# Skip factors of a state-space block: four columns become four rows before they go to DRAM, and the loads of them move

## The chip, the cores and the metric

The kernel runs on one core of a Trainium2 chip. The metric is the device time of one execution in microseconds, smaller is better. Three runs of the kernel before gave 994.62, 995.08 and 999.35 us; the median is 995.08.

## The reference

A block of two parts on 2048 tokens of width 640, with a modulation computed from a conditioning vector `c`:

```
mod = (silu(c) @ w_mod)                       # sa, ca, ga, sb, cb, gb, each 640 long
h = layernorm(x) * (1 + ca) + sa
x = x + ga * A(h)                             # A: long convolution by FFT, plus h * Dskip
h = layernorm(x) * (1 + cb) + sb
x = x + gb * B(h)                             # B: (h Wg * h Wu) Wd

K[d, l] = Re sum_n C[d,n] * exp(dt[d]*(A_re + i A_im)[d,n] * l) * dt[d]*B[d,n]
A(h) = causal convolution of h with K, plus h * Dskip
```

`Dskip` is added to tap 0 of the convolution kernel, scaled as the kernel itself is (by `ga` and `1 + ca`). These scaled values are the skip factors.

## The kernel before

The work has two big stages. Up to about 480 us the kernel generates the convolution kernels K and runs the FFT convolution of part A; behind that, the matmuls of part B. The channels go in five blocks of 128, NB = 5. K is generated in 40 steps n of 16 channels each: GpSimd builds phase and magnitude tables (Ph, EQ, EP: L710), ScalarE takes absolute values and sines of them (ab, tra, trb: all ScalarE work stands at L230, in a helper), VectorE multiplies (QtA, PtA, QtB, PtB: L765 to L792), TensorE multiplies the halves (kg: L807 and L822) and adds the skip factors of every second step by one matmul of `dskt` with the identity (L811).

Each step has three groups, and between the groups stand slots for side jobs. A job has due times in the table SCHED; a slot runs the jobs that are due in order of their numbers. So the order of instructions on each engine is written at build time, and each engine works through its list in order. An instruction that waits holds everything behind it on its engine. SP issues nearly all transfers in this way, in one list.

Side jobs that matter here:

- `mod_l` and `u_modr`/`u_modc`: load a 1600 KB piece of `w_mod` into t_tw or t_ti (L353) and multiply it with silu(c) (L360).
- `u_stats`: load rows of A_u into buffers gha, ghb, ghc and others (L465), take their statistics on VectorE (L473). `row_stats` makes reciprocal standard deviations of them (L276 to L283).
- `u_hm`: normalise those rows on ScalarE and store them in DRAM as `hm` (L485); rows whose buffer had to be given away are loaded again first (L465 too). A buffer can be loaded again only when its store has landed.
- `u_pre`: load `hm` back, transposed by the access pattern (L856), and start the FFT.
- `u_fold`, due at 157, 189, 197 and 222: TensorE turns modulation rows into columns (L379), VectorE combines them (L384 to L396), among them the skip factors `dcol[:, 1:]`, 128 channels by 4 blocks. SP stores these in DRAM, `dgd` (L397). TensorE then spreads the columns sh and gg over all rows by products with the identity (L403, L404), and ScalarE copies the results from PSUM into shr and f16a.
- `dskip(j)`, four jobs: load `dgd` into partition 32 j of `dskt`, 32 runs of 4 values each (L413). Channel block 0 (n below 8) uses values loaded at the start; the blocks behind it need these loads from n = 9 on.
- `u_k`: the first FFT step of a finished K (L844), copied to f16b by ScalarE.

A transfer of a column layout such as `dgd[P:].rearrange("(b p) -> p b")` moves single values of 4 bytes.

Of the kernel before, what the change touches and what calls it, by code (L numbers as in the profile page):

```python
# [18 lines left out]
P = 128  # L19
D = 640  # L20
# [3 lines left out]
NB = D // P  # L24
# [46 lines left out]
    tab=(487, 829),  # L71
    fo=(157, 189, 197, 222),
    e0=(138,),
    ds=(205, 222, 503, 397),
    mc=((-872, 289, 307, 356, 356), (217, 378, 439, 446, 461), (309, 570, 620)),
    q=(
# [148 lines left out]
def tile_kernel(ctx: ExitStack, tc: tile.TileContext, I, out):  # L225
    nc = tc.nc
    V, S, G, PE, SY = nc.vector, nc.scalar, nc.gpsimd, nc.tensor, nc.sync

    def act(o, i, f=AF.Copy, **kw):
        return S.activation(o, i, f, **kw)  # L230
# [12 lines left out]
    ident = const.tile([P, P], F32, name="ident")  # L243
# [17 lines left out]
    def ring(pool, shape, name, dtype=F32):  # L261

        return pool.tile(shape, dtype, name=name + next(slot[name]), bufs=1)
# [3 lines left out]
    def mark(*k):  # L267
        done[k] = done.get(k, 0) + 1

    def need(n, *k):  # L270

        assert done.get(k, 0) >= n, k
# [63 lines left out]
    tv0, tv1 = (ring(fp, [P, 1024], "TV") for _ in range(2))  # L336
    CH = (slice(0, 384), slice(384, D))
    row = [[tv0[0:1, 0:384], tv0[0:1, 384:D]], [tv1[0:1, 0:384], tv1[0:1, 384:D]], [tv0[0:1, D:], tv1[0:1, D : D + 256]]]
    mcol = kconst.tile([P, 5, NB], F32, name="mcol")
    dcol = kconst.tile([P, NB], F32, name="dcol")  # L340
    dgd = dram1.tile([D], F32, name="dgd")
# [31 lines left out]
    def u_fold():  # L373

        need(6, "row")
        pc = ring(ps_f, [P, 512], "psf")
        for m in range(3):
            for b in range(NB):
                PE.matmul(pc[:, m * NB + b : m * NB + b + 1], row[m][b // 3][:, b % 3 * P : b % 3 * P + P], ident[0:1, 0:1], start=True, stop=True)  # L379
        yield  # L380
        p3 = pc[:, : 3 * NB].rearrange("p (m b) -> p m b", m=3)
        sg, rg, g1, sh, gg = (mcol[:, i, :] for i in range(5))
        gp_, gq = pc[:, 16 : 16 + NB], pc[:, 24 : 24 + NB]
        V.tensor_scalar(gp_, p3[:, 1], 1.0, 2.0, op0=OP.add, op1=OP.mult)  # L384
        V.tensor_scalar(sg, gp_, 0.0, 0.5, op0=OP.is_ge, op1=OP.subtract)
        V.tensor_tensor(gp_, gp_, sg, op=OP.mult)
        V.tensor_scalar(gp_, gp_, 1e-20, 2.0, op0=OP.max, op1=OP.mult)
        V.tensor_tensor(g1, gp_, sg, op=OP.mult)
        V.tensor_tensor(gp_, gp_, sg, op=OP.mult)
        V.reciprocal(rg, gp_)  # L390
        V.tensor_tensor(gq, p3[:, 2], g1, op=OP.mult)
        V.tensor_tensor(gg[:, 0:1], p3[:, 2, 0:1], g1[:, 0:1], op=OP.mult)
        V.tensor_tensor(sh[:, 1:], p3[:, 0, 1:], rg[:, 1:], op=OP.mult)
        V.scalar_tensor_tensor(sh[:, 0:1], p3[:, 0, 0:1], rg[:, 0:1], gg[:, 0:1], op0=OP.mult, op1=OP.mult)
        V.tensor_tensor(dt2[:, 1:], gq[:, 1:], dt2[:, 1:], op=OP.mult)
        V.tensor_tensor(dcol[:, 1:], gq[:, 1:], dcol[:, 1:], op=OP.mult)  # L396
        SY.dma_start(dgd[P:].rearrange("(b p) -> p b", p=P), dcol[:, 1:])  # L397
        mark("gg")
        yield
        pt, ps = (ring(ps_f, [P, 512], "psf") for _ in range(2))  # L400
        for b in range(NB):
            o = pt[:, 0:P] if b == 0 else ps[:, (b - 1) * P : b * P]
            PE.matmul(o, sh[:, b : b + 1].to_broadcast([P, P]), ident, start=True, stop=True)  # L403
        PE.matmul(pt[:, P : 2 * P], gg[:, 0:1].to_broadcast([P, P]), ident, start=True, stop=True)  # L404
        yield
        act(shr[:, 0:P], pt[:, 0:P])
        act(xa[:, 4, 0:P], pt[:, P : 2 * P])
        act(shr[:, P:], ps)
        mark("sh")

    def dskip(j):
        need(1, "gg")
        SY.dma_start(dskt[32 * j : 32 * j + 1, 8:], dgd[P:].rearrange("(o t j l) -> o j t l", o=1, j=4, l=4)[:, j])  # L413
        mark("dsk")

# [855 lines left out]
    at(T0["tab"][:1], once(tables))  # L1271
    at(T0["tab"][1:], once(tables_b))
    at(T0["fo"], u_fold)
    at(T0["e0"], once(lambda: LATE.pop()()))
    for j in range(4):
        at(T0["ds"][j : j + 1], once(dskip), j)
# [375 lines left out]
    for r in range(3):  # L1652
        b = (1, 13, 25)[r]
# [192 lines left out]
```

## Time and profile before

| | before |
|---|---|
| runs | 994.62, 995.08, 999.35 us |
| median | 995.08 us |
| profiled execution, its time | 996.15 us |
| profiled execution, its span | 994.4 us |
| granted TensorE clock, mean | 0.95 |
| busy PE, DVE, ACT, POOL | 90%, 73%, 58%, 51% |
| shares of the chain that ended last | PE 55%, DVE 14%, ACT 12%, issue 10%, DMA 6%, POOL 2% |
| moved | 188.54 MB in 159337 packets, 10352 of them under 512 B |

The span is counted from the first to the last instruction; the time has some 1.75 us more around it. Rows of a timeline give start, duration, engine, line, operation, output and inputs, and in square brackets how long the engine was idle before and what ended that. SPq is SP's list of transfers: its durations are those of issuing, and "DMA" in a chain is the time from the issue to the landing. PE, DVE, ACT and POOL are TensorE, VectorE, ScalarE and GpSimd; PEld is TensorE's weight load. Line numbers in the text are those of the kernel before.

### The profile page before, as it was taken

To read this page: it belongs to the slowest core of one execution; us is meant where nothing else is said; L and a number is where in the kernel's file an instruction comes from. 1 tells how busy PE (TensorE), PEld (TensorE's weight loads), DVE (VectorE), ACT (ScalarE), POOL (GpSimd) and SP (SyncE) were. 2 spreads that over 40 slices of the span, in tenths; PEclk is the share of its full clock that TensorE was granted. 3 is DMA by queue.
4 is the path that set the end of the run, shared out by engine and by line. 5 is a ranking of instruction groups with operands and counts; after the bars stand their busy time and mean duration, and the time that the engine had idled before them with its cause. 6 is when DMAs were issued, how large, how long until landed. Compare 5 with 4: busy or idle time off the path is not lost.

```text
span 994.4 us, 26747 instructions
## 1 busy us (share of the span) xinstructions
PE 893.7 (90%) x11120; PEld 725.3 (73%) x11120; DVE 729.1 (73%) x1408; ACT 577.0 (58%) x1071; POOL 510.8 (51%) x400
## 2 busy tenths in 40 slices
PE   4867898899889689998877999999999999999998
PEld 3565656676576567777635888889999788888998
DVE  8798569889989887894758655566677656568952
ACT  4869989886978878772345333334455443435430
POOL 5978899799779989950030254440113122222110
PEclk9877889899889889999999899999999999999999
DMA  8728654555246443667685565724564577658875
GB/s 262 257 54 303 219 186 136 177 167 173 77 153 194 138 123 121 188 214 236 208 230 202 172 214 187 238 92 147 155 241 114 193 228 236 217 181 290 238 239 186
DMA packets 159337, 188.54 MB, mean 190 GB/s; under 512 B 10352, under 2 KB 128880, under 8 KB 158064
## 3 DMA queue, kind: packets, MB, share of 16 engines
q1 hardware_dynamic: 150000, 155.51, 48.8%
q0 software_dynamic: 4752, 21.63, 7.5%
q10 hardware_dynamic: 4464, 9.70, 2.6%
q8 instruction: 87, 1.43, 0.6%
q14 instruction: 34, 0.28, 0.1%
HBM read 124.22 MB, written 62.59 MB: 188 GB/s over the span
## 4 chain that ended last, share of the span: by engine, by line
PE 55%; DVE 14%; ACT 12%; issue 10%; DMA 6%; POOL 2%; SPq 1%; DVEq 0%; POOLq 0%; ACTq 0%
PE pa L1074 17%; PE pa L1508 9%; PE psg L1074 8%; PE psfc L889 2%; PE kg L822 2%; PE kg L807 2%; PE psfa L889 2%; ACT L230 1%; PE psfb L889 1%; ACT trb L230 1%; DMA TVa<-WD 1%; PE psfb L946 1%; PE pa L1560 1%; ACT tra L230 1%; PE psfc L946 1%
## 5 line engine op out<-in xcount | busy, mean ns | idle before, releaser
L1051 POOL TENSOR_TENSOR tf<-wur,wgb 128x256 f32<-128x256 f32 x23 | 18.2, 792 | 251.7 <-DVE wtl L1022 204.5
L710 POOL TENSOR_TENSOR EQ<-LQ,RH 128x1536 f32<-128x1536 f32 x40 | 124.2, 3105 | 9.8 <-DVE QtB L767 9.6
L1022 DVE TENSOR_TENSOR wtl<-tf,wth 128x256 fp32r<-128x256 f32 (+1 forms) x72 | 36.6, 509 | 58.9 <-ACT wth L230 58.9
L710 POOL TENSOR_TENSOR Phb<-LH,DH 128x1536 int32<-128x1536 int32 x20 | 62.3, 3114 | 13.5 <-ACT tra L230 13.5
L710 POOL TENSOR_TENSOR EP<-LP,RH 128x768 f32<-128x768 f32 x40 | 66.0, 1651 | 0.0
L710 POOL TENSOR_TENSOR Pha<-LH,DH 128x1536 int32<-128x1536 int32 (+1 forms) x21 | 62.4, 2971 | 2.9 <-ACT trb L230 2.6
L1508 PE MATMUL pa<-wsg,sh 128*128 128x384 f32 (+1 forms) x304 | 58.6, 311 | 0.0
L822 PE MATMUL kg<-QtB,PtB 64*32 64x64 f32 x2560 | 48.5, 229 | 5.9 <-DVE QtB L766 5.3
L822 PEld LDWEIGHTS kg<-QtB,PtB 64*32 64x32 f32 x2560 | 41.5, 114 | 16.0 <-issue 7.1
L1508 PEld LDWEIGHTS pa<-wsg,sh 128*128 128x128 f32 x304 | 45.8, 189 | 0.0
L1547 POOL DMA_DIRECT2D wsg<-wdc x21 | 11.2, 532 | 66.5 <-PE pa L1560 35.5
L1022 DVE TENSOR_TENSOR wsg<-wga,wsg 128x640 fp32r<-128x640 f32 x36 | 32.9, 920 | 11.9 <-ACT wsg L230 11.9
L1074 PE MATMUL pa<-sh,wth 128*128 128x512 f32 x112 | 35.3, 397 | 6.5 <-DVE a L1423 6.1
L1022 DVE TENSOR_TENSOR sl<-a,sh 128x512 fp32r<-128x512 f32 x53 | 36.7, 712 | 5.8 <-ACT sh L230 5.8
L230 ACT ACTIVATE sh<-a 128x512 fp32r<-128x512 f32 x53 | 32.0, 622 | 14.9 <-PE psg L1560 6.2
L230 ACT ACTIVATE a<-pa 128x512 f32<-128x512 f32 x12 | 7.2, 597 | 54.7 <-PE pa L1074 54.7
L230 ACT ACTIVATE wsg<-wga 128x640 fp32r<-128x640 f32 x36 | 26.1, 729 | 21.7 <-PE pa L1508 11.0
L230 ACT ACTIVATE wth<-tf 128x256 fp32r<-128x256 f32 (+1 forms) x72 | 32.2, 479 | 9.8 <-PE pa L1074 5.3
L1074 PE MATMUL pa<-hh,wsg 128*128 128x512 f32 x136 | 36.7, 395 | 0.5 <-DVE wsg L1022 0.5
L1139 POOL TENSOR_SCALAR hfa<-xb,hr,hr 128x128 f32<-128x128 f32 x4 | 2.3, 572 | 67.6 <-DVE hr L283 67.6
L230 ACT ACTIVATE s<-pa 128x512 f32<-128x512 f32 x11 | 6.6, 598 | 49.4 <-PE pa L1074 49.4
L765 DVE TENSOR_TENSOR QtA<-tra,EQ 128x1024 f32<-128x1024 f32 x20 | 24.4, 1221 | 14.8 <-PE kg L807 9.2
(665 smaller groups left out, 3143.8 us busy)
## 6 DMA issues: line engine op xcount, KB each, us to landing
wsg<-wdc POOLq DMA_DIRECT2D x21, 640.0 KB, 5.1
wgb<-B_w_gate SPq DMA_DIRECT2D x24, 320.0 KB, 4.7
wur<-B_w_up SPq DMA_DIRECT2D x24, 320.0 KB, 6.0
wsd<-wsg SPq DMA_DIRECT2D x12, 640.0 KB, 3.9
wga<-wdg SPq DMA_DIRECT2D x12, 640.0 KB, 4.6
wsg<-wsd POOLq DMA_DIRECT2D x12, 640.0 KB, 4.7
wdc<-xb SPq DMA_DIRECT2D x21, 320.0 KB, 4.2
TVb<-WD SPq DMA_DIRECT2D x22, 256.0 KB, 3.5
```

What stands on the lines that cost most here:

```text
L230: return S.activation(o, i, f, **kw)
L710: G.tensor_tensor(o.rearrange("p x (h l) -> p x h l", l=8), lo.unsqueeze(2).to_broadcast([P, rows, nh, 8]), hi.rearrange("p h x -> p x h") ...
L765: return [lambda: V.tensor_tensor(Qt[:, :, :, 0:32], tr[:, :, :, ::-1], e[:, :, 0:32].unsqueeze(1).to_broadcast([P, 2, R, 32]), op=OP.mult ...
L807: PE.matmul(kg[j * 32 : j * 32 + 32, dd, :], PtA[:, c, dl * 4 + j, :], QtA[:, c, dl * 4 + j, :], start=dd == 0 and c == 0, stop=False, til ...
L822: PE.matmul(kg[j * 32 : j * 32 + 32, dd, :], PtB[lo : lo + 64, c, r, :], QtB[lo : lo + 64, c, r, :], start=False, stop=dd == 7 and c == 1, ...
L889: PE.matmul(r[c][par * 64 : par * 64 + 64, i, :], t_tw[:, k0 + k, c, :], src[:, k, :], start=True, stop=True, tile_position=(0, par * 64))
L946: PE.matmul(r[par][:, i], t_ti[lo : lo + 64, qd * 4 + i, c, :], x[lo : lo + 64, c, i, :], start=c == 0, stop=c == 1, tile_position=(lo, 0))
L1022: V.tensor_tensor(lo, v, hi, op=OP.subtract)
L1051: E.tensor_tensor(t[:, 0:2], u[:, 0:2], g[:, 0:2], op=OP.subtract)
L1074: PE.matmul(ps, w[a][:, k], x[b][:, l], start=first and n == 0 and m == 0, stop=n == 2 and m == len(ks) - 1, skip_group_check=True)
L1508: PE.matmul(AC[tb][t][c], x[:, ts], w[:, cs], start=st, stop=f == NF - 1 and n == 2 and (c == 0 or t % 2 == 1))
L1547: G.dma_start(WD[q], wdc[:, q // 3, q % 3])
```

## The change

The store of the skip factors moves from the second piece of `u_fold` to its last one. Before it TensorE multiplies `dcol[:, 1:]` with the identity into four rows of 128 values, next to the products of L403 and L404, and ScalarE copies these rows from PSUM into a free part of buffer TVb. The store then has four pieces of 512 bytes. The due times of the four loads change from 205, 222, 503, 397 to 250, 255, 397, 411.

```diff
-    ds=(205, 222, 503, 397),
+    ds=(250, 255, 397, 411),
...
+    drow = tv1[0 : NB - 1, D + 256 : D + 256 + P]
...
         V.tensor_tensor(dcol[:, 1:], gq[:, 1:], dcol[:, 1:], op=OP.mult)
-        SY.dma_start(dgd[P:].rearrange("(b p) -> p b", p=P), dcol[:, 1:])
         mark("gg")
         yield
...
         PE.matmul(pt[:, P : 2 * P], gg[:, 0:1].to_broadcast([P, P]), ident, start=True, stop=True)
-        yield
+        PE.matmul(pt[0 : NB - 1, 2 * P : 3 * P], dcol[:, 1:], ident, start=True, stop=True)
+        yield
+        act(drow, pt[0 : NB - 1, 2 * P : 3 * P])
+        SY.dma_start(dgd[P:].rearrange("(b p) -> b p", p=P), drow)
+        mark("dg")
         act(shr[:, 0:P], pt[:, 0:P])
...
     def dskip(j):
-        need(1, "gg")
+        need(1, "dg")
```

On SP, at the place where `u_fold` ends, this stood in a row before (the last row is the load that waits for the store of ghc):

```order
L397 DMA dgd<-dcol 128x4x1
L413 DMA dskt<-dgd 1x32x4
L353 DMA t_tw<-w_mod 128x5x640
L413 DMA dskt<-dgd 1x32x4
L465 DMA ghb<-A_u 128x640
L485 DMA hm<-f16a 128x640
L485 DMA hm<-Wb 128x640
L485 DMA hm<-Wa 128x640
L485 DMA hm<-ghc 128x640
L465 DMA ghc<-A_u 128x640
```

And this stands there now (the lines of the changed file are four further down, `TVb` is the buffer with the four rows):

```order
L354 DMA t_tw<-w_mod 128x5x640
L408 DMA dgd<-TVb 4x128
L469 DMA ghb<-A_u 128x640
L489 DMA hm<-f16a 128x640
L489 DMA hm<-Wb 128x640
L417 DMA dskt<-dgd 1x32x4
L489 DMA hm<-Wa 128x640
L417 DMA dskt<-dgd 1x32x4
L489 DMA hm<-ghc 128x640
L469 DMA ghc<-A_u 128x640
```

The load of t_tw is now ahead of the store, three transfers stand between the store and the first load of it where none stood, and the first two loads stand among the stores of `hm`. The other two loads, which stood nine transfers apart, now stand together at the place of the first.

On TensorE, the rows of `u_fold` before, with the products of a finished step around them:

```order
L403 MATMUL psfb<-ident,mcol 128x128
L403 MATMUL psfc<-ident,mcol 128x128 x4
L404 MATMUL psfb<-ident,mcol 128x128
L822 MATMUL kg<-QtB,PtB 32x64 x32
L844 MATMUL psfb<-ct,Kta 64x128 x8
```

And now:

```order
L403 MATMUL psfb<-ident,mcol 128x128
L403 MATMUL psfc<-ident,mcol 128x128 x4
L404 MATMUL psfb<-ident,mcol 128x128
L405 MATMUL psfb<-ident,dcol 4x128
L826 MATMUL kg<-QtB,PtB 32x64 x32
L848 MATMUL psfb<-ct,Kta 64x128 x8
```

One product is added ahead of those of the step. ScalarE gets one copy, TVb from psfb, ahead of the copies into shr and f16a. VectorE and GpSimd keep their order.

## The prediction

> **What bounds the kernel now.** First the page's busy shares, then a table of stages, then the chain of work that ended last, then the waits of SP's queue and of ScalarE. No single engine bounds the kernel; the share changes with the stage, so the change has to be priced in the stage in which it acts, 60 to 125 us. From the table by stages (length, then busy us of PE, PEld, DVE, ACT, POOL, the granted clock, the DMA share, GB/s):
>
> ```profile
> 59.00:62.40 3.40, 0.63 (x7) 0.23 (x3) 3.06 (x18) 1.83 (x4) 3.16 (x6) 0.50 0.36 96
> 62.80:71.60 8.80, 8.22 (x170) 7.10 (x169) 7.58 (x21) 4.75 (x10) 6.32 (x3) 0.74 0.07 5
> 79.00:86.00 7.00, 4.67 (x73) 2.79 (x72) 5.77 (x14) 6.46 (x11) 5.44 (x3) 0.85 0.87 319
> ...
> 75.00:92.00 17.00, 12.71 (x219) 8.91 (x219) 14.84 (x29) 15.92 (x27) 13.35 (x6) 0.80 0.88 297
> 92.00:112.00 20.00, 16.41 (x188) 10.65 (x188) 10.92 (x21) 19.82 (x39) 15.58 (x17) 0.59 0.65 224
> 112.00:124.00 12.00, 10.52 (x314) 8.80 (x310) 9.45 (x16) 11.84 (x21) 11.97 (x5) 1.00 0.90 273
> ```
>
> ScalarE is the limit from 75 to 112 us (15.92 of 17 busy, then 19.82 of 20), and GpSimd takes over from 112 (11.97 of 12). What ScalarE loses between 75 and 112 therefore moves everything behind it; what another engine or a queue loses there costs nothing until ScalarE or GpSimd waits for it. Between 62.8 and 71.6 the DMA engines are nearly empty (share 0.07, 5 GB/s), and from 79 to 86 nearly full (0.87, 319 GB/s).
>
> The reason stands in the waits of SP's queue and in its timeline:
>
> ```profile
> SPq L413 <- DMA dgd<-dcol: 8.7, 1, 8.7
> SPq L465 <- DMA hm<-ghc: 6.5, 1, 6.5
> ```
> ```profile
> 58.75 0.33 SPq L465 DMA_DIRECT2D ghc<-A_u  x1
> 62.44 0.38 SPq L397 DMA_DIRECT2D dgd<-dcol  x1
> 71.66 0.56 SPq L413 DMA_DIRECT2D dskt<-dgd  x1
> 72.32 2.50 SPq L353 DMA_DIRECT2D t_tw<-w_mod  x1
> 74.87 0.53 SPq L413 DMA_DIRECT2D dskt<-dgd  x1
> 75.50 0.52 SPq L465 DMA_DIRECT2D ghb<-A_u  x1
> 76.07 0.52 SPq L485 DMA_DIRECT2D hm<-f16a  x1
> 77.19 0.32 SPq L485 DMA_DIRECT2D hm<-Wb  x1
> 78.00 0.32 SPq L485 DMA_DIRECT2D hm<-Wa  x1
> 78.82 0.32 SPq L485 DMA_DIRECT2D hm<-ghc  x1
> 85.68 0.33 SPq L465 DMA_DIRECT2D ghc<-A_u  x1
> ```
>
> SP issues the skip store at 62.44 and then stands for 8.7 us at the first load of it. The big weight load t_tw, queued behind, starts only at 72.32, and runs into the stores of normalised rows; the store hm<-ghc at 78.82 takes until 85.68 to land, and the next row load waits for it. In the chain this shows as 10 us of transfers:
>
> ```profile
> 62.33 0.80 PE psfb L403 x2
> 64.83 0.43 PE psfb L404 x2
> 65.26 1.86 PE kg L822 x64
> 67.12 1.21 PE psfb L844 x16
> 68.36 0.60 ACT f16b L230
> 78.82 6.84 DMA hm<-ghc
> 85.68 3.29 DMA ghc<-A_u
> 89.05 0.92 ACT ghc L230
> 112.03 2.59 POOL Pha L710
> ```
>
> But a chain says only what came last at each step. What ScalarE did while those transfers ran is in its own rows; these are the rows from 64 to 93 us in which it was idle:
>
> ```profile
> 67.18 0.36 ACT L230 ACTIVATE ptb<-ptb 128x192 f32<-128x192 f32 x1 [0.32 <-issue]
> 68.36 0.60 ACT L230 ACTIVATE f16b<-psfb 128x512 f32<-128x512 f32 x1 [0.57 <-PE psfb L844]
> 71.82 0.21 ACT L230 ACTIVATE ry<-rv 128x10 f32<-128x10 f32 x1 [1.35 <-DVE rv L276]
> 82.51 0.93 ACT L230 ACTIVATE ghb<-ghb,nm,rs 128x640 f32<-128x640 f32 x1 [0.45 <-DMA ghb<-A_u]
> 89.05 0.92 ACT L230 ACTIVATE ghc<-ghc,nm,rs 128x640 f32<-128x640 f32 x1 [0.42 <-DMA ghc<-A_u]
> ```
>
> ScalarE waited for transfers only twice, 0.45 us at 82 and 0.42 us at 89. The rest of the 10 us lay beside work that it had to do anyway.
>
> **The change part by part.** *What goes.* The 8.7 us stand of SP goes: t_tw now follows the row load of 58.75 directly. What it overwrites was last read much earlier, and DMA is idle then. It is issued at about 58.75 + 0.33 = 59.1 and, by its row below, lands 8.0 us later, near 67. The row load ghb, which waits for the statistics taken from its old contents, is free well before 75.50:
>
> ```profile
> 68.41 0.88 DVE L473 BATCH_NORM_STATS2 st<-ghb 128x6 f32<-128x320 f32 x2
> t_tw<-w_mod SPq DMA_DIRECT2D x3, 1600.0 KB, 8.0
> ghc<-A_u SPq DMA_DIRECT2D x7, 320.0 KB, 4.1
> ```
>
> So ghb can start near 69.4 and is there in time for 82: ScalarE's wait of 0.45 us goes.
>
> *The two loads of skip factors* now stand between the stores, one behind hm<-Wb and one behind hm<-Wa. With what is added below (0.43), hm<-Wb goes out at 77.62, the load at 77.94 (0.56), hm<-Wa at 78.50, the second load at 78.82 (0.56), hm<-ghc at 79.38 instead of 78.82. The landing of hm<-ghc is what I choose: all stores into hm took
>
> ```profile
> DMA to landing us min/median/max: 2.7/4.5/7.2
> ```
>
> With t_tw gone from that stretch I take the median, 4.5; the load behind it starts at 83.9 and with 4.1 us is there at 88.0. ScalarE asks for it at 89.05 - 0.42 - 0.45 + 0.43 = 88.61. So the second wait, 0.42 us, goes too, with 0.6 us to spare. [...]
>
> *The store itself.* SP waits with it for ScalarE's copy, about 66.2; behind it stand ghb (free at 69.4) and hm<-f16a (76.07 so far). If the four pieces landed no faster than the old store, 66.2 + 8.7 = 74.9, still before the first load at 77.9: that cost is zero at both ends.
>
> *What TensorE gets.* One more product, dcol by ident, behind the one of L404 and ahead of kg L822, on the chain. The trace has no product with four output rows; the nearest row is L404, the same shape of moving operand, 0.43 us until the next. Bounds: 0, if four columns of weights let it slip in, and 0.80, the L403 pair that starts from standstill. I take 0.43. It is paid: L822, L844 and ScalarE's f16b at 68.36, which waits for L844, all move by it. [...]
>
> *What ScalarE gets.* One copy of 4x128 ahead of the copies of shr. The nearest row is the 128x128 copy:
>
> ```profile
> 65.94 0.26 ACT L230 ACTIVATE shr<-psfb 128x128 f32<-128x128 f32 x1
> ```
>
> 0.26 us, covered by the 0.32 and 0.57 us in which ScalarE stood at 67.18 and 68.36; without that cover it would be 0.26 on the chain. Its input is there at 65.26 + 0.43 = 65.69, before 65.94, so the copies behind it don't wait for TensorE either.
>
> *The other two loads* go out together behind the row load of 111 us instead of at 111.7 and 120.3: one more issue of 0.5 us ahead of the stores of 113 us, for which no engine waits at once; zero, at most 0.5.
>
> Sum: +0.43 - 0.45 - 0.42 = **-0.44 us**. Against the profiled execution: span 994.4 becomes 994.0, time 996.15 becomes 995.7. That execution lies 1.07 above the median of the runs (995.08), so the median forecast is **994.6**. Bounds: -0.87 (both waits gone, nothing paid) to +1.06 (0.80 and 0.26 paid, no wait gone).
>
> **The rivals.** *The store hm<-ghc lands as late as before (slower).* If the crowd at 79 to 86 us is the row stores and loads rather than t_tw, 6.84 stays: load at 79.38 + 6.84 = 86.22, there 3.33 later (85.68 to 89.01 now) at 89.55, ScalarE waits 0.94 instead of 0.42. Sum: +0.43 - 0.45 + 0.52 = +0.50, time 995.6. It decides from the point at which store and load together take over 88.61 - 79.38 = 9.2 us; before they took 10.1. For it: two loads in small pieces stand among the stores now, and the median would leave only 0.6. Against it: 1600 KB leave the stretch.
>
> *The stand of SP counts in full (faster).* If the 8.7 us came off the chain, 8.7 - 0.43 = 8.3 us would go, 986.8. For it: 10 us of transfers stand in the chain. Against it: ScalarE's busy 15.92 of 17 and 19.82 of 20; nothing can be taken from a busy engine by moving a transfer.
>
> *Nothing is gained since the store is as slow as before* ends at the forecast: nobody waits for it until 77.9.
>
> **How the numbers follow.** A run here can tell about 0.5%, 5 us, from no change. Forecast 0.72; late store 0.18; SP's stand in full 0.06; 0.04 for something behind 144 us that a shift of half a microsecond brings into collision, worth over 5 us (one of the three runs before was 999.35). So faster 0.06, same 0.90, slower 0.04. Range: the bounds give 994.2 to 996.1; the distance between the profiled execution and the median (1.07) shows what one median may miss by, and I allow one and a half of it: 992.6 to 997.7.
>
> **What would show it.** Right: t_tw issued near 59 us; no wait for dgd on SP; ScalarE without waits for ghb and ghc between 75 and 92; the chain through TensorE at 65 longer by about 0.4. Wrong: a wait of SP at the loads of dgd; ScalarE still waiting at 89 (late store); or ScalarE reaching its last sine ahead of GpSimd's 112 us more than 2 us earlier (SP's stand in full); a changed time with those steps unchanged would mean a stage that I did not look at.

## The result, and the profile after

Seven runs of each kernel were timed. The change took 989.64 to 994.91 us, median 990.9; the kernel before 993.44 to 999.35, median 996.29. The ratio is 0.9953 (95% interval 0.9930 to 0.9976): 5 us faster where the forecast said 0.4, and below the forecast range. Five further comparisons, below, gave ratios of 0.9984 to 1.0009. Most of the 5 us was not seen again.

The profiled execution of the change took 990.9 us with a span of 989.1. SP's timeline shows the new order at work (start, us, queue, line, transfer):

```profile
58.41 0.39 SPq L354 DMA_DIRECT2D t_tw<-w_mod  x1
65.46 0.28 SPq L408 DMA_DIRECT2D dgd<-TVb  x1
68.56 0.36 SPq L469 DMA_DIRECT2D ghb<-A_u  x1
...
76.31 0.56 SPq L417 DMA_DIRECT2D dskt<-dgd  x1
76.92 0.57 SPq L489 DMA_DIRECT2D hm<-Wa  x1
77.53 0.52 SPq L417 DMA_DIRECT2D dskt<-dgd  x1
78.15 0.54 SPq L489 DMA_DIRECT2D hm<-ghc  x1
80.56 0.33 SPq L469 DMA_DIRECT2D ghc<-A_u  x1
```

The stand of 8.7 us is gone: t_tw goes out at 58.41 instead of 72.32 and the row load ghb at 68.56 instead of 75.50. From the issue of hm<-ghc to that of the load behind it pass 2.41 us; before, 6.86. ScalarE's rows in the same stretch:

```profile
66.96 0.58 ACT L230 ACTIVATE f16b<-psfb 128x512 f32<-128x512 f32 x1
69.01 0.21 ACT L230 ACTIVATE ry<-rv 128x6 f32<-128x6 f32 x1 [0.17 <-DVE rv L276]
70.56 0.21 ACT L230 ACTIVATE ry<-rv 128x10 f32<-128x10 f32 x1 [1.34 <-DVE rv L276]
80.74 0.91 ACT L230 ACTIVATE ghb<-ghb,nm,rs 128x640 f32<-128x640 f32 x1
86.78 0.91 ACT L230 ACTIVATE ghc<-ghc,nm,rs 128x640 f32<-128x640 f32 x1
```

Neither ghb nor ghc carries a wait any more: both are gone, as forecast. In the table by stages ScalarE fills 16.79 of the 17 us from 75 to 92, where it had filled 15.92, and the DMA share there falls from 0.88 to 0.52:

```profile
75.00:92.00 17.00, 12.86 (x186) 8.88 (x174) 15.57 (x30) 16.79 (x28) 14.62 (x7) 0.79 0.52 177
```

But f16b, which waited 0.57 us for TensorE before, now waits for nothing, although TensorE has one product more. That was not forecast. The next section asks how large the gain really is and where the added product went.

### The profile page after: what moved, and what is told of

The parts are those of the page before. It is cut to its first block, busy times and chain, and to the rows that moved or that the text cites. A ratio compares the mean times of both kernels' runs of the same rounds, so it can differ in the third digit from the quotient of the medians.

```text
span 989.1 us, 26749 instructions
## 1 busy us (share of the span) xinstructions
PE 891.2 (90%) x11122; PEld 722.0 (73%) x11122; DVE 730.0 (74%) x1408; ACT 576.5 (58%) x1072; POOL 509.6 (52%) x400
## 3 DMA queue, kind: packets, MB, share of 16 engines
q8 instruction: 87, 1.43, 0.6%
## 4 chain that ended last, share of the span: by engine, by line
PE 53%; DVE 16%; ACT 12%; issue 10%; DMA 6%; POOL 2%; SPq 1%; DVEq 0%; POOLq 0%; ACTq 0%
PE pa L1078 18%; PE pa L1512 9%; PE psg L1078 8%; PE psfc L893 2%; PE kg L811 2%; PE psfb L893 2%; PE psfa L893 2%; PE kg L826 1%; ACT tra L230 1%; ACT trb L230 1%; ACT L230 1%; DMA xsb<-A_u 1%; PE psfc L950 1%; DVE QtA L769 1%; PE pa L1564 1%
## 5 line engine op out<-in xcount | busy, mean ns | idle before, releaser
L1078 PE MATMUL pa<-sl,wth 128*128 128x512 f32 x112 | 35.0, 394 | 0.0
```

The costliest lines, as they stand in the source:

```text
L1078: PE.matmul(ps, w[a][:, k], x[b][:, l], start=first and n == 0 and m == 0, stop=n == 2 and m == len(ks) - 1, skip_group_check=True)
```

## The experiments

**How large is the gain?** The unchanged kernel before and the changed one were run again.

> The changed kernel once more. Theory A (SP's stand of 8.7 us is the cause: 0.87 us directly at ScalarE, and the rest by the clock that TensorE is granted behind it): ratio to before 0.995 to 0.997, again a higher mean granted clock than before (0.957 against 0.950 in the first pair of traces). Rival D (the draws of the clock differed by luck, the change itself is worth the -0.44 us of the forecast): ratio 0.999 to 1.000, and the same mean clock as before.

> The kernel before, unchanged, against itself: what the comparison shows where nothing differs, and a second trace of it. The first comparison of the change gave 0.9953 from seven runs each, a second one with twelve runs 0.9984. Theory E (a few runs of each kernel spread by some 10 us, so that the first comparison overstated an effect of 1 to 2 us): ratio within 0.998 to 1.002 and a spread of 987 to 1000 us. In the trace, the half-clock stretches of TensorE between 48 and 110 us lie elsewhere than in the first trace of the same kernel, and ScalarE waits again for the row loads ghb and ghc, 0.3 to 0.6 us each; if they lie at the same place, the change itself moves them.

> The changed kernel, to settle the size. Theory A (5 us): 0.995 to 0.997. Forecast (-0.44) or theory E (1 to 2 us): 0.998 to 1.000.

> The changed kernel once more, as the one two runs before: the size, and another trace, in which the half-clock stretches between 48 and 110 us, and at 190 and 320 us, lie where the phase of the clock puts them, not where the change does.

> The change again, for the size. By the path in the traces (0.8 to 1.0 us earlier on ScalarE at 87 us in every trace of the change, nothing further that does not move between runs of one kernel): 0.5 to 1.5 us below the kernel before. By the first comparison (seven runs each): 4 to 5 us below. By the third and fourth: no difference.

> The change again, for the size: 0.4 to 1.0 us below the kernel before by the path (0.56 between the two traces in which TensorE was at half clock at 65 us, 0.8 between two at full clock); 4 to 5 us by the first comparison.

Each row below stands beside runs of the kernel before on the same chip: 35 for the second set, the same 29 for the third, the fourth and the last row, 35 for the fifth and 29 for the sixth. These 128 runs come from four chips.

| runs | median us | before, median | ratio (95% interval) |
|---|---|---|---|
| change again, 12 | 992.16 | 993.72 | 0.9984 (0.9963 to 1.0006) |
| change, third, 12 | 993.64 | 994.23 | 1.0002 (0.9979 to 1.0024) |
| change, fourth, 12 | 994.34 | 994.23 | 0.9992 (0.9971 to 1.0013) |
| change, fifth, 12 | 994.39 | 994.23 | 1.0009 (0.9989 to 1.0029) |
| change, sixth, 12 | 993.98 | 994.17 | 0.9992 (0.9973 to 1.0012) |
| kernel before against itself, 12 | 993.98 | 994.23 | 0.9996 (0.9979 to 1.0012) |

The 60 runs of the change have a mean of 993.89, the 128 of the kernel before 994.25: 0.36 us less, with a standard error of 0.41, so that it can't be told from nothing. With the first seven of each the difference is 0.70, standard error 0.40. One run scatters by a standard deviation of 2.3 (before) to 2.8 us (change), and by up to 10.5 us within one set of twelve. The forecast's 0.44 lies well inside both; the 5 us of the first comparison does not. What set those seven apart isn't settled. The mean granted clock alone doesn't explain it: it was 0.958 over those seven runs of the change, and 0.957 over the twelve of the sixth set, whose ratio is 0.9992.

**Where did the cost of the product go?** The same places differ between two traces of one kernel, depending on whether TensorE was granted half or full clock at 62 to 67 us. The windows of 62 to 67 us say which (length, busy us of PE, PEld, DVE, ACT and POOL, granted clock, DMA share, GB/s). Of the kernel before, first and second profile:

```profile
62.00:67.00 5.00, 4.67 (x76) 4.33 (x76) 4.93 (x14) 2.05 (x5) 5.00 (x3) 0.50 0.07 5
```
```profile
62.00:67.00 5.00, 3.54 (x93) 3.06 (x92) 4.93 (x11) 3.63 (x10) 5.00 (x3) 1.00 0.07 5
```

The first profile of the change had 1.00 there, the fifth 0.50:

```profile
62.00:67.00 5.00, 3.72 (x94) 3.04 (x93) 4.93 (x11) 3.79 (x11) 5.00 (x3) 1.00 0.50 198
```
```profile
62.00:67.00 5.00, 4.56 (x59) 3.91 (x63) 4.93 (x14) 2.08 (x6) 5.00 (x3) 0.50 0.68 268
```

So the two profiles that stood beside each other at first were of different clocks at this place. (In the change's second profile the added product took 0.38 us, as in the first, where the clock was 1.00; in the third, fourth and sixth the pair of L403 took 0.49 us, as in the first, and the product behind it 0.59, as in the fifth, where the clock was 0.50.) Like must be set beside like. For that a kernel is needed with the loads late and no product, which was run twice; its second run had the half clock (0.50 at 62 to 67 us):

> The kernel before with the new due times of the four loads alone: the store keeps its pieces of 4 bytes and its old place, TensorE and ScalarE get nothing added. Theory A: SP no longer stands, t_tw is issued near 63 us, ratio 0.995 to 0.997, no slower than the full change. Rival B (the pieces of 4 bytes themselves cost, wherever the loads stand): ratio 0.999 to 1.001. Rival D: 0.999 (only 0.87 us).

> The loads alone moved later, with the store of 4-byte pieces at its old place and no product on TensorE, for the size. If the order of the loads is the whole effect, as much below the kernel before as the change itself (0.5 to 1.5 us); if the rows through TensorE bring something of their own, less than the change by over 1 us.

On the kernel before:

```diff
-    ds=(205, 222, 503, 397),
+    ds=(250, 255, 397, 411),
```

At half clock, the fifth profile of the change, from the timelines of TensorE and ScalarE:

```profile
62.44 0.79 PE L403 MATMUL psfb<-ident,mcol 128*128 128x128 f32 x2 [2.83 <-DVE mcol L395]
65.30 0.59 PE L405 MATMUL psfb<-ident,dcol 128*4 128x128 f32 x2
65.82 1.92 PE L826 MATMUL kg<-QtB,PtB 64*32 64x64 f32 x64
67.67 1.09 PE L848 MATMUL psfb<-ct,Kta 128*64 128x128 f32 x16
68.81 0.60 ACT L230 ACTIVATE f16b<-psfb 128x512 f32<-128x512 f32 x1 [0.91 <-PE psfb L848]
88.49 0.91 ACT L230 ACTIVATE ghc<-ghc,nm,rs 128x640 f32<-128x640 f32 x1
```

and the second profile with the loads alone:

```profile
62.34 0.80 PE L403 MATMUL psfb<-ident,mcol 128*128 128x128 f32 x2 [2.77 <-DVE mcol L394]
65.20 1.93 PE L822 MATMUL kg<-QtB,PtB 64*32 64x64 f32 x64
67.07 1.26 PE L844 MATMUL psfb<-ct,Kta 128*64 128x128 f32 x16
68.38 0.60 ACT L230 ACTIVATE f16b<-psfb 128x512 f32<-128x512 f32 x1 [0.57 <-PE psfb L844]
88.06 0.91 ACT L230 ACTIVATE ghc<-ghc,nm,rs 128x640 f32<-128x640 f32 x1
```

ScalarE normalised ghc at 89.05 in the first profile of before, at 88.06 with the loads alone and at 88.49 with the change. At half clock the loads bring 0.99 and the product takes 0.43 back, the size of the forecast's term (0.33, if counted from the start of L403, which differs by 0.10). That it agrees so closely is partly luck: on TensorE the product took 0.52 (65.30 to 65.82), and the FFT step behind it took 0.17 less (1.09 us instead of 1.26). The change is worth 0.56 there, 0.67 from the start of L403; the forecast said 0.44.

At full clock, the first profile of the change:

```profile
61.57 0.49 PE L403 MATMUL psfb<-ident,mcol 128*128 128x128 f32 x2 [0.26 <-DVE mcol L395]
63.10 0.38 PE L405 MATMUL psfb<-ident,dcol 128*4 128x128 f32 x2
63.42 1.10 PE L826 MATMUL kg<-QtB,PtB 64*32 64x64 f32 x64
65.80 1.09 PE L848 MATMUL psfb<-ct,Kta 128*64 128x128 f32 x16 [1.28 <-ACT f16a L230]
```

and the second of the kernel before:

```profile
61.65 0.49 PE L403 MATMUL psfb<-ident,mcol 128*128 128x128 f32 x2 [0.27 <-DVE mcol L394]
65.74 1.09 PE L844 MATMUL psfb<-ct,Kta 128*64 128x128 f32 x16 [1.46 <-ACT f16a L230]
81.22 0.92 ACT L230 ACTIVATE ghb<-ghb,nm,rs 128x640 f32<-128x640 f32 x1 [0.34 <-DMA ghb<-A_u]
87.62 0.92 ACT L230 ACTIVATE ghc<-ghc,nm,rs 128x640 f32<-128x640 f32 x1 [0.28 <-DMA ghc<-A_u]
```

Here TensorE stands before the FFT step (L844, now L848) for ScalarE's f16a, 1.46 us without the product and 1.28 with it: TensorE is no longer on the chain, and the product, 0.32 us there (63.10 to 63.42), is free. The two waits are smaller here, 0.34 and 0.28. ghc moves from 87.62 to 86.78, 0.84 us, or 0.76 from the start of L403.

Half clock alone does not make the product cost something. In the third, fourth and sixth profile of the change it took 0.59 us too, but L403 began over 1 us earlier, at 60.8 to 61.2. There f16b waited 0.16 us or not at all, ScalarE waited 0.34 to 0.85 for rv instead, and ghc came at 86.80 to 86.84.

**How far does the gain reach?** GpSimd's tables behind it show that. At Pha, near 110 us, the change is 0.65 us ahead of the kernel before in the half-clock pair (111.38 against 112.03) and 0.87 in the full-clock pair (109.64 against 110.51). At Phb, near 180, it is 0.28 behind in the one (180.89 against 180.61) and 0.79 ahead in the other (178.64 against 179.43). So the gain at ghc need not reach the end of the kernel.

**Is the product covered, and by how much?** It was issued eight times instead of once:

> The change with its added TensorE product issued eight times instead of once. One took 0.38 us at full clock and 0.59 at half, in the traces of the change; seven more are 2.2 to 4.1 us on TensorE at 64 us. Theory (the added product was free because VectorE's rv at 68 us cannot end before GpSimd's Phb, near 69.1, in any trace, so there are 0.3 to 1.7 us of cover): the seven use the cover up and show the rest. ScalarE's first square root starts at 69.7 to 72 instead of 69.2 and ScalarE normalises ghc at 87.3 to 89.5 instead of 86.9; the time is 0.5 to 3 us above the change. Rival, the product is on the chain and paid in full as the forecast had it: 2.2 to 4.1 us later at both places. Rival, TensorE is off the chain here: both places stay at 69.2 and 86.9.

```diff
-        PE.matmul(pt[0 : NB - 1, 2 * P : 3 * P], dcol[:, 1:], ident, start=True, stop=True)
+        for _ in range(8):
+            PE.matmul(pt[0 : NB - 1, 2 * P : 3 * P], dcol[:, 1:], ident, start=True, stop=True)
```

TensorE's and ScalarE's rows of that profile, at full clock (the pair of L403 took 0.49 us):

```profile
63.12 1.91 PE L406 MATMUL psfb<-ident,dcol 128*4 128x128 f32 x16
65.99 1.09 PE L849 MATMUL psfb<-ct,Kta 128*64 128x128 f32 x16
67.13 0.60 ACT L230 ACTIVATE f16b<-psfb 128x512 f32<-128x512 f32 x1
86.93 0.91 ACT L230 ACTIVATE ghc<-ghc,nm,rs 128x640 f32<-128x640 f32 x1
```

Eight took 1.91 us, so seven more took 1.53, not the 2.2 to 4.1 expected. L849 comes 0.19 us later than in the change and without a wait; ghc moves by 0.15. The 1.28 us of TensorE's wait took in nearly all of it. Even the 0.15 need not be the products' doing, since GpSimd's Phb, 0.03 us behind whose end rv ends here (see below), begins 0.14 later in this trace too (65.98 against 65.84). The median was 996.19, ratio 1.0013 (0.9993 to 1.0032), not told apart from the kernel before.

**A second cover, on VectorE.** In the traces at full clock the first square root, ry, waits for VectorE's rv, which belongs to 128x6 values and yet takes up to 1.86 us. VectorE, GpSimd and ScalarE with the loads late, first profile:

```profile
67.30 1.86 DVE L276 TENSOR_SCALAR rv<-mv 128x6 f32<-128x6 f32 x1
66.02 3.12 POOL L710 TENSOR_TENSOR Phb<-LH,DH 128x1536 int32<-128x1536 int32 x1
69.19 0.21 ACT L230 ACTIVATE ry<-rv 128x6 f32<-128x6 f32 x1 [1.74 <-DVE rv L276]
```

rv ends at 69.16, 0.03 us behind GpSimd's instruction (the rounded figures give 0.02), and so it does in each of the eleven traces in which it begins before that end. In two forms GpSimd's Phb was to be held back by a small copy ahead of it that reads nm. A first attempt had the copy at the wrong place, behind Phb, due at t of 114 instead of 11, and so was the change once more with one small instruction added (995.07 us, ratio 1.0012, 0.9990 to 1.0034):

> The change with GpSimd's table product Phb (3.1 us, from 66.0 to 69.1 before) held back behind the first reciprocal root: a copy of six columns of nm1 on GpSimd stands ahead of it. GpSimd has 5 us of idle time behind Phb. Theory (VectorE's rv is held until GpSimd's instruction ends): with GpSimd idle rv takes 0.12 to 0.2 us instead of 0.3 to 1.9, ScalarE's first square root starts at its table load's end or at rv's, 67.7 to 68.9 instead of 69.2, the second about 1.5 us behind it, and ScalarE normalises ghc 0.3 to 1.5 us earlier than 86.9; the time is 0 to 1.5 us below the change, unless Phb, now at 69 to 73, holds other instructions of VectorE instead. Rival (rv is late for its own input or VectorE's order): the first square root stays at 69.2, Phb starts near 70.6, nothing is gained.

The two others had it at the right place, with the change and with the loads alone:

> The change with GpSimd's product Phb of 66 us held back behind both reciprocal roots, now at the right place: a copy of six columns of nm1 on GpSimd, that of the second root, stands ahead of it, so that Phb starts near 70 to 71. GpSimd has 5 us of idle time there. Theory (VectorE's rv at 68 cannot end before GpSimd's instruction does, and that is what hid the added product): where TensorE runs at full clock at 62 to 66, rv takes 0.12 to 0.2 us wherever it starts, ScalarE's first square root comes at the end of its table load or of rv, 67.7 to 69.0 instead of 69.1 to 69.4, and ScalarE normalises ghc at 85.4 to 86.7 instead of 86.8 to 87.1; the time is 0 to 1.5 us below the change. Rival (rv is late for its own input): it stays long or the root stays at 69.2, and ghc at 86.9. If TensorE falls into half clock there (first square root at 70.7, ghc at 88.5 in the fifth run of the change), rv is short in any case and this run tells nothing.

> The kernel before with the loads of the skip factors later (4-byte store as before, no product on TensorE) and Phb held back as in the run above: both costs gone. ScalarE normalises ghc at 85.3 to 86.6 at full clock, 88.0 at half clock. 1 to 2.5 us below the kernel before if the theory of the hold is right, 0.5 to 1.5 otherwise; the fastest of all the forms, if by little.

```diff
+        if t == 11:
+            G.tensor_copy(ryw[:, 16:22], nm1[:, 6:12])
         if g < 2 and n + 1 < NK:
             kg_pool(n + 1, g)
```

The first of these ran at half clock at this place (the pair of L403 took 0.79 us) and tells nothing, as its expectation says. The second ran at full clock (0.49):

```profile
68.62 0.12 DVE L277 TENSOR_SCALAR rv<-mv 128x6 f32<-128x6 f32 x1
72.03 3.10 POOL L711 TENSOR_TENSOR Phb<-LH,DH 128x1536 int32<-128x1536 int32 x1
68.78 0.21 ACT L230 ACTIVATE ry<-rv 128x6 f32<-128x6 f32 x1
86.68 0.92 ACT L230 ACTIVATE ghc<-ghc,nm,rs 128x640 f32<-128x640 f32 x1
```

With GpSimd idle rv takes 0.12 us, and ry begins at 68.78 rather than 69.0 to 69.4. That agrees with the theory. The long hold of 1.7 us was not met without Phb, since rv began late in this run; ghc came at 86.68, not at the 85.3 to 86.6 expected. The times were 993.28 (0.9983, 0.9965 to 1.0001) and 993.92 (1.0001, 0.9979 to 1.0022): neither can be told from the change, and no faster form was found.

**The parts of the change.** The rows through TensorE with the loads at their first two old places, and with the other two alone at theirs:

> The changed kernel with the first two loads right behind the store and the last two at their old due times (222, 222, 503, 397). It measures how long the store in four pieces takes until a load may follow: by the nearest rows 2.7 to 4.5 us instead of 8.7. SP then stands from about 65.7 to 69 us, but t_tw is ahead of it. Theory A: 0.995 to 0.997, since t_tw leaves early all the same. Rival B: the same. Rival C (the last two loads' place matters): 0.999 to 1.000.

> The changed kernel with the third load back at its old due time (250, 255, 503, 397), so that the last two loads stand apart as before. Theory A: as the full change, 0.995 to 0.997. Rival C: 0.999 to 1.000, and the lead over before behind 120 us is smaller than with the pair together.

The edits of the change, rows only and then pair back:

```diff
-    ds=(250, 255, 397, 411),
+    ds=(222, 222, 503, 397),
```

```diff
-    ds=(250, 255, 397, 411),
+    ds=(250, 255, 503, 397),
```

Rows only, SP's timeline: the loads stand right behind the store, and yet SP waits little, 0.9 us from the end of the store's issue to the first load, not the 2.7 to 4.5 expected.

```profile
64.35 0.28 SPq L408 DMA_DIRECT2D dgd<-TVb  x1
65.54 1.20 SPq L417 DMA_DIRECT2D dskt<-dgd  x2
67.44 0.36 SPq L469 DMA_DIRECT2D ghb<-A_u  x1
```

From the start of the store's issue to that load pass 1.19 us with four pieces of 512 bytes; with 512 pieces of 4 bytes 9.22 passed in the kernel before (62.44 to 71.66). ghc is normalised at 86.94 here, at 86.96 with the loads alone (first run), at 86.78 to 86.96 in the change's profiles without a wait of f16b: rows alone and later loads alone each remove the stand, and the whole is worth no more than either. The other two loads go out behind 109 us, so that ghc says nothing of them. GpSimd's Phb behind them begins at 178.75 with the pair back, and at 178.45 to 180.89 in the six profiles of the change. The times were 992.77 (0.9994, 0.9974 to 1.0015), 992.17 (0.9986, 0.9965 to 1.0008), and with the loads alone 992.01 (0.9984, 0.9963 to 1.0005) and 993.86 (0.9992, 0.9970 to 1.0013).

**Does the stand count in full?** The kernel before with a second store of 4-byte pieces and a load of it, ahead of the first:

> The kernel before with a second stand of SP: the skip factors are stored into a scratch buffer in pieces of 4 bytes, loaded from there into a free part of TVb (which nothing reads), and only then stored and loaded as before. SP stands about 8.7 us longer, t_tw is issued near 81 us, ghb near 84. If ScalarE's need at 82 and 89 us decides (the view of the forecast: the first 8 of the 8.7 us were free), this second stand has no cover left: ScalarE waits 7 to 10 us for ghb and the time goes up by 6 to 9 us, ratio 1.006 to 1.009. If the first stand cost 5 us of 8.7 (theory A), the second would cost at least as much in proportion, 5 us or more; if transfers are of no concern to ScalarE there, nothing.

```diff
+        SY.dma_start(dge[P:].rearrange("(b p) -> p b", p=P), dcol[:, 1:])
+        SY.dma_start(tv1[0:1, D + 256 : D + 256 + P].rearrange(...), dge[P:].rearrange(...)[:, 0])
         SY.dma_start(dgd[P:].rearrange("(b p) -> p b", p=P), dcol[:, 1:])
```

SP's waits in that kernel (total us, times, longest):

```profile
SPq L416 <- DMA dgd<-dcol: 10.2, 1, 10.2
SPq L399 <- DMA dge<-dcol: 8.4, 1, 8.4
```

Its timelines of SP and ScalarE:

```profile
85.61 1.08 SPq L354 DMA_DIRECT2D t_tw<-w_mod  x1
94.41 0.92 ACT L230 ACTIVATE ghb<-ghb,nm,rs 128x640 f32<-128x640 f32 x1 [12.31 <-DMA ghb<-A_u]
```

It took 12.4 us more (1006.6 against 994.23; ratio 1.0129, 1.0103 to 1.0154), not the 6 to 9 expected, because this second store and its load cost SP more than the first 8.7. The second stand moves t_tw back by 13.29 us, from 72.32 to 85.61, and ScalarE's wait for ghb grows by 11.86, from 0.45 to 12.31. So in the kernel before nearly all of the cover was used up: of the first stand 0.87 us showed at ScalarE, of a second one almost all.

## Why the prediction was wrong, point by point

**What held.** t_tw goes out at 58.41 (forecast 59.1). The wait for dgd is gone. Both waits of ScalarE are gone, in each of the traces of the change. The landing behind hm<-ghc was forecast as 4.5 us; from its issue to the next load passed 2.77 to 4.92 in the three traces with late loads and the store in 4-byte pieces (4.27 in the one above, 79.53 to 83.80) and 2.4 in all six profiles of the change. So the late store, 6.84, is refuted. ScalarE's added copy, 0.25 us, is covered as forecast. The other two loads show no cost: with them at their old places the median was 992.17, with the change 992.16 on the same chip. SP's stand in full is refuted too: without it ScalarE comes to ghc 0.56 to 0.84 us earlier, not 8.3.

**What failed, first: the term of +0.43 for the product, "it is paid".** On TensorE the product took 0.52 us at half clock and 0.32 at full, where the prediction had 0.43; whether it is paid depends on who waits for whom. At half clock ScalarE's ghc came 0.43 later with it than with the loads alone. Of the traces, though, only five of seventeen show f16b waiting 0.5 us or more for TensorE: the first of before, that with the second stand, the fifth of the change, the second with the loads alone, and the change with Phb held back. In the rest f16b waits 0.16 us or not at all, and in nearly all of them TensorE waits for ScalarE's f16a or ScalarE for rv, so that the term is 0. In the first trace of the kernel before the granted clock was 0.50 from 62.33, where L403 begins, to 67.4, with TensorE busy throughout (5.07 of 5.07 us); what begins or ends such a stretch was not shown. In the full-clock pair ghc came 0.84 earlier, where the forecast had 0.44: 0.62 are the two waits, and nothing was paid for the product. This step is worth 0.4 us and does not explain the miss.

**What failed, second: the step that took the range from three runs.** The distance of the profiled execution from the median of three (1.07), one and a half times, was to show what a median may miss by. Medians of the same changed kernel ranged from 990.9 to 994.39 in six sets of seven or twelve. Five of the six lie between 992.1 and 994.4, the kernel before's later medians between 993.72 and 994.23, and not at 995.08; the range from 992.6 up held four of the six. A standard deviation of 2.3 to 2.8 us for one run makes 0.9 to 1.1 for the mean of seven, and as much for the one it is compared with. The range of the forecast was too narrow for any kernel with this scatter.

**What failed, third: the sum put everything behind 144 us at nothing,** but for a chance of 0.04 of a collision. Two of GpSimd's instructions, of the first profile of before and of the change, show what lay there:

```profile
180.61 3.12 POOL L710 TENSOR_TENSOR Phb<-LH,DH 128x1536 int32<-128x1536 int32 x1 [4.09 <-ACT tra L230]
504.05 0.88 POOL L1139 TENSOR_SCALAR hfa<-xb,hr,hr 128x128 f32<-128x128 f32 x2 [67.64 <-DVE hr L283]
```
```profile
178.64 3.12 POOL L714 TENSOR_TENSOR Phb<-LH,DH 128x1536 int32<-128x1536 int32 x1 [4.55 <-ACT tra L230]
499.82 0.88 POOL L1143 TENSOR_SCALAR hfa<-xb,hr,hr 128x128 f32<-128x128 f32 x2 [67.29 <-DVE hr L283]
```

These two executions are 2.27 us apart at ghc (the two profiles of the kernel before are 1.43 apart there), 1.97 at Phb, 4.23 at hfa and 5.3 at the end. So 3.3 of the 5.3 us arose behind 180 us, where the change moves no instruction: the last load of skip factors goes out at 120.30 in the kernel before and at 109.20 in the change. From Phb to hfa the six profiles of the change took 320.8 to 327.1 us, the two of the kernel before 323.4 and 321.9. This stretch alone differs by more from run to run than the change is worth, and a forecast of the time needs it in its range.

**What stays open.** The first comparison lies 4 us from the later five, more than the scatter of its seven runs makes likely. Both sides of it were unusual: the seven runs of the kernel before have a mean of 996.22, 2.0 above the later 128, and the seven of the change 991.60, 2.3 below the later 60. No step of the change was found that gives more than 0.99 us at ScalarE's ghc. What makes the stretch from 180 to 500 us longer or shorter was not tested, and whether the first seven runs stood on one of the four chips of the later sets is not known. The gain that the experiments support is 0.56 to 0.84 us at the place; in the time of the later sets it is 0.36 with an error of 0.41, which can't be told from nothing.

## What to carry to other kernels

A long wait of a queue is worth only what the bound engine behind it waits, here 0.6 to 0.9 of 8.7 us; adding a second such wait on purpose shows how much cover was left. When the granted clock moves from run to run, compare two traces only where they had the same clock in the stage in question, and ask of each added instruction whether its engine is waited for in both. When a time differs by more than the change can give, follow a few instructions along both profiles and see where they draw apart. Take the range of a forecast from the scatter of single runs and the number that will be timed, and have more than three before saying that a kernel's time is known to 1 us.

## What the runs showed of the hardware

A VectorE instruction of 128x6 values took from 0.12 to 1.86 us, according to when it began, and ended 0.03 us behind the end of GpSimd's 3.1 us instruction in each of the eleven traces in which it began before that. VectorE's product with a PSUM operand (PtAb) took 1.22 us in the middle of the same GpSimd instruction (66.52 to 67.74 in the change's first profile, inside 65.84 to 68.95) and 1.22 with GpSimd idle (66.45 to 67.67, with the loads late and Phb held back). With GpSimd idle the 128x6 instruction took 0.12 us (68.62, the same trace). This agrees with its being held until GpSimd's instruction ends; what would hold it, and why it does not hold PtAb, was not shown.

Half-clock stretches of TensorE fell differently from run to run of one kernel: in the first profile of before, 62 to 67 us was wholly at 0.50, in the second at 1.00. The expectation of the change's fourth run has a phase of the clock put them where they lie; no run shows one. Between these two profiles, with nothing else changed, ScalarE's ghc lay 1.43 us apart (89.05 and 87.62), more than the change moved it; 0.68 of that was there already at the start of L403 (62.33 and 61.65).
